# Pooled attention with a soft mixture of experts: another order for the end of the attention, and a tail in quarters of columns

## The chip, the cores and the metric

One core of a Trainium2 chip runs one program. TensorE (PE; PEld is its loading of weights) multiplies, VectorE (DVE) and ScalarE (ACT) work on its sums in PSUM and on SBUF, GpSimd (POOL) on SBUF alone, and SyncE (SP) issues the transfers. Each works through its own instructions in order; semaphores keep them in step. The metric is the device time of one execution, in microseconds (us), as the median of several.

## What is computed

The reference, cut to what matters. Eight batches of eight heads; the queries are averaged in pairs, so 576 of them meet 1152 keys. The result is a table x of 4608 rows and 512 columns, which goes through a soft mixture of 8 experts with 4 slots each.

```python
q_pool = q.reshape(B, H, S // 2, 2, D).mean(axis=3)
scores = scale * q_pool @ k.T
attn = exp(scores - scores.max(-1)); attn /= attn.sum(-1) + 1e-09
x = (attn @ v)                       # 4608 x 512
logits = x @ phi                     # 4608 x 32
d = exp(logits - logits.max(0)); d /= d.sum(0) + 1e-09
slot_input = d.T @ x                 # 32 x 512
slot_out[e] = relu(slot_input[e] @ w1[e]) @ w2[e]     # 8 experts, 4 slots each
c = exp(logits - logits.max(1)); c /= c.sum(1) + 1e-09
return c @ slot_out                  # 4608 x 512
```

All of it is in fp32.

## The kernel before

The attention runs in 96 units: 32 pairs of heads by three thirds of 192 queries. For a unit, PE makes the scores of nine blocks of 128 keys (`S`), ACT copies them, DVE takes the maximum, PE turns it (`mt`, `mb`), DVE and POOL subtract it, ACT takes exponentials, and PE multiplies with v (`av`). Three units' results of four pairs make a batch of x, `xn`.

Each of the eight batches then goes through its part of the mixture (class `Moe`): `xa` and `xb` turn `xn`, `lg` makes the logits in four groups of 32 rows, one for each pair of heads, `to` adds the groups with the matrix `SI4f` (one half holds two of the three thirds, the other the third one, so there are two `lg` and two `to`), `rm` and `nm` take the running maximum over all rows, `ex` the exponentials. `we` (method `weights`, line 803) turns these exponentials, so that they can be the stationary side of the gather: for each of the three thirds a block of 128 rows, which goes to `eA`, and a rest of 64, which is written twice, to the upper and the lower 64 partitions, and goes to the two halves of `eB`. `ga` (method `gather`, line 829) multiplies them with x, with three groups of 32 columns of the array at work at once, and adds the sum to `slot`, rescaled by `corr`. `cb`, `ce`, `cy`, `cz`, `cr` and `cm` make the combine weights `cN`.

What sets the order: every engine's instructions stand as they are issued (class `InOrder`, line 380). Up to the last `av` a planner (`graph`, `plan`) sets the order from a table of costs and due times; what is left then, the end of batch 6 (b) and all of batch 7 (a), is ordered by hand in `end` (line 353): a list of steps, each with the PSUM bank that it uses. A step with a phase 0 is PE's part, one with a phase 1 or more the copy or sum that takes it out of PSUM. Bank numbers 0 to 7 lie in four tiles of two banks; waits are kept by tile.

Behind the attention lies the tail. `pT` turns `slot` and divides it by the sums (`SIz`), DVE copies it to `sT`, and the experts run: `up` (first weights, 512 columns), `relu`, `turn_h`, `down` (second weights; four experts at once in four groups of 32 columns, twice). `down` goes by halves h of the 512 output columns. `spread` copies a half's sum and spreads it over the partitions; `give` multiplies it with the turned combine weights `cT` (made by `turn_c` in three blocks of 16) and writes pieces of 384 kB. Each `give` makes two writes. The expert weights are 64 tiles of 512 kB; NW = 28 of them have buffers of their own and are loaded during the attention, NW2 = 20 take over the attention's memory, and the last 16 take the first 16's buffers.

Of the kernel before, what the change touches and what calls it, by code (L numbers as in the profile page):

```python
# [352 lines left out]
def end(B, u):  # L353
# [10 lines left out]
        (("lg", a, 1, 0), 2), (("lg", a, 1, 1), 2),  # L364
        (("to", a, 0, 0), 0), (("rm", a, 0), None),
        (("to", a, 1, 0), 6), (("rm", a, 1), None),
        (("we", b, 0), 4), (("nm", a), None), (("we", b, 3), 4), (("ex", a), None), (("we", b, 2), 4),
        (("we", a, 0), 2), (("we", a, 2), 2), (("we", a, 3), 2),
        (("ns", a), None), (("zs",), None), (("to", a, 0, 1), 0), (("to", a, 1, 1), 6),
        (("ga", b, 0), 4), (("ga", b, 1), 4), (("ga", b, 2), 4),  # L370
        (("ga", a, 0), 2), (("ga", a, 1), 2), (("ga", a, 2), 2),
        (("cb", a, 0), 6), (("cb", a, 1), 6), (("ce", a), None), (("cy", a), None), (("cz", a), None), (("cr", a), None), (("cm", a), None),
# [3 lines left out]
NW2 = 20  # L376
NW = 28
# [18 lines left out]
def pooled_attention_soft_moe(ctx: ExitStack, tc: tile.TileContext, q, k, v, phi, w1, w2, out):  # L396
# [44 lines left out]
    cN = keep.tile([NQ, NT, NS], F32, name="cN")  # L441
    slot = keep.tile([P, DM], F32, name="slot")
# [217 lines left out]
    class Moe:  # L660
# [195 lines left out]

    pairs = [Pair(n) for n in range(B * HP)]
# [3 lines left out]
    def load_first(i):  # L861
# [19 lines left out]
        ga=lambda i, *a: M_(i).gather(*a), zs=lambda _: total_sum(), w=lambda i, _: load_first(i),  # L881
# [21 lines left out]
    cT = tl.tile([P, NT // 4, NQ], F32, name="cT")  # L903

    def turn_c(k, bank):

        for i in range(4):
            t = 16 * k + 4 * i
            pe.transpose(bank[:, i * NQ:(i + 1) * NQ], cN[:, t:t + 4, :].rearrange("p t s -> p (t s)"), ident[:NQ, :NQ])
        act.copy(cT[:, 4 * k:4 * k + 4, :], bank[:, :4 * NQ].rearrange("p (t n) -> p t n", t=4))  # L910

    pT = banks[4]
    for c in range(KC1):
        pe.matmul(pT[:, c * NS:(c + 1) * NS], slot[:, c * P:(c + 1) * P], SIz, start=True, stop=True)
    sT = tl.tile([P, KC1, NS], F32, name="sT")
    dve.tensor_copy(sT, pT[:, :KC1 * NS].rearrange("p (c s) -> p c s", c=KC1))

# [29 lines left out]
    DH = DM // 2  # L947

    def down(h, r, i, cs=range(4)):

        for c in cs:
# [5 lines left out]
    so = [tl.tile([P, DH], F32, name=f"so{h}") for h in range(2)]  # L957

    def spread(h, phase):

        if phase == 0:
            last[h] = tl.tile([P, DH], F32, name=f"last{h}")
            act.copy(last[h], banks[h][:, :DH])
        else:
            pe.matmul(banks[2 + h][:, :DH], SI4f, last[h], start=True, stop=True)
            dve.tensor_copy(so[h], banks[2 + h][:, :DH])

    last = {}

    def give(h, k, fc):  # L970

# [4 lines left out]
        for x in range(2):  # L976
            ob = ring([P, 2, 4 * NQ], F32, f"ob{h}_{k}_{fc}_{x}")
            for t in range(2):
                (act.copy if t else dve.tensor_copy)(ob[:, t], pts[2 * x + t])
# [71 lines left out]
```

## Time and profile before

| | us |
|---|---|
| median of 3 timed runs | 885.15 |
| lowest and highest | 882.51, 886.06 |
| profiled execution, own time | 887.7 |
| its span, first to last instruction | 885.9 |
| mean granted TensorE clock in the span | 0.989 |

A profile is one execution, recorded by the hardware. Busy time of an engine is the time in which one of its instructions runs; matmuls overlap, so a group's busy time ends with its last one's end. In a row of the timeline stand the start, the busy time, the engine, the operation, the tile written and those read, and how many instructions were merged; in brackets, for how long the engine had idled and what ended that. `f32` products take two passes each and count twice; turns take one. All instructions of the kernel carry line 390, that of the helper which records them, so they are told apart by tiles: `d` and `b` are PSUM, in the attention and in the tail.

### The profile page before, as it was taken

What the parts mean: (1) busy time and instruction counts of PE and PEld (TensorE: products, weight loads), DVE (VectorE), ACT (ScalarE), POOL (GpSimd) and SP (SyncE); (2) the same over time, 40 slices, a digit from 0 to 9 for tenths busy, and PEclk for the clock granted to TensorE, in tenths of its full rate; (3) what the DMA queues carried; (4) which work ended last, traced back from release to release, by engine and by line L of the source; (5) the groups of instructions that cost most, each with busy time, mean ns of one, the idle gap of its engine ahead of it and who ended that gap; (6) DMA issues with size and microseconds to landing.
All of it is one profiled execution on the core that took longest, in us unless ns stands there. A gap on an engine that the chain in (4) does not pass through costs nothing.

```text
span 885.9 us, 36358 instructions
## 1 busy us (share of the span) xinstructions
PE 844.9 (95%) x16240; PEld 705.1 (80%) x16240; DVE 745.4 (84%) x1090; ACT 754.7 (85%) x1142; POOL 351.3 (40%) x244
## 2 busy tenths in 40 slices
PE   5999999999999999999999999999999999998995
PEld 4888888887888878887888878887888878887342
DVE  5899999997999979998899979998899979995223
ACT  5899899998899989998899989998899989997123
POOL 1444444442444434443444434444344423441100
PEclk9999999999999999999999999999999999999898
DMA  6143434341333334341243332221132222217688
GB/s 166 56 130 106 130 107 130 106 131 29 117 120 104 108 104 131 107 130 29 84 126 106 107 82 82 83 82 30 56 84 82 83 63 74 72 69 277 267 330 329
DMA packets 102428, 102.08 MB, mean 115 GB/s; under 512 B 78336, under 2 KB 78848, under 8 KB 102272
## 3 DMA queue, kind: packets, MB, share of 16 engines
q1 hardware_dynamic: 102272, 99.76, 36.4%
q8 instruction: 127, 2.08, 1.0%
q14 instruction: 29, 0.24, 0.1%
HBM read 90.31 MB, written 9.44 MB: 113 GB/s over the span
## 4 chain that ended last, share of the span: by engine, by line
PE 63%; ACT 25%; issue 7%; DVE 4%; DMA 0%; SPq 0%; DVEq 0%; ACTq 0%
PE d L390 57%; ACT s L390 20%; PE b L390 5%; DVE M L390 2%; ACT mS L390 1%; ACT Us L390 1%; ACT lT L390 1%; ACT xT L390 1%; DVE s L390 1%; DMA k<-in_k_dram 0%; DVE rc L390 0%; DVE d L390 0%; DVE mc L390 0%; ACT eB L390 0%; ACT eA L390 0%
## 5 line engine op out<-in xcount | busy, mean ns | idle before, releaser
L390 PE MATMUL d<-qs,k 64*128 64x192 f32 x3456 | 367.9, 342 | 14.1 <-DMA k<-in_k_dram 5.0
L390 ACT COPY s<-d 128x768 f32<-128x768 f32 (+1 forms) x480 | 334.5, 737 | 45.5 <-PE d L390 38.8
L390 PEld LDWEIGHTS d<-v,s 128*64 128x64 f32 x10368 | 319.0, 138 | 51.3 <-issue 28.1
L390 PE MATMUL d<-v,s 128*64 128x65 f32 x10368 | 346.9, 224 | 8.5 <-ACT lT L390 5.4
L390 ACT ACTIVATE s<-s 128x1152 f32<-128x1152 f32 x288 | 328.6, 1169 | 7.1 <-DVE s L390 6.1
L390 POOL TENSOR_TENSOR s<-s,mS 128x1152 f32<-128x1152 f32 x95 | 251.8, 2651 | 196.7 <-issue 109.3
L390 PEld LDWEIGHTS d<-qs,k 64*128 64x128 f32 x3456 | 275.1, 188 | 47.7 <-ACT s L390 18.3
L390 DVE TENSOR_TENSOR s<-s,d 128x1152 f32<-128x1152 f32 x193 | 259.5, 1346 | 7.5 <-PE d L390 4.4
L390 DVE TENSOR_TENSOR M<-d,M 128x768 f32<-128x768 f32 (+1 forms) x288 | 237.1, 823 | 25.6 <-ACT s L390 11.2
L390 POOL TENSOR_TENSOR xn<-Us,rc 128x192 f32<-128x192 f32 x95 | 48.3, 508 | 171.3 <-DVE rc L390 113.2
L390 DVE TENSOR_TENSOR M<-d,s 128x768 f32<-128x768 f32 x96 | 91.0, 948 | 15.5 <-ACT s L390 14.9
L390 DVE TENSOR_TENSOR d<-d,M 128x384 f32<-128x384 f32 x96 | 54.4, 567 | 21.5 <-ACT s L390 12.3
L390 POOL TENSOR_TENSOR qs<-qs,q 128x576 f32<-128x576 f32 x31 | 44.1, 1422 | 38.4 <-DMA q<-in_q_dram 32.0
L390 DVE TENSOR_REDUCE mc<-d 128x3 f32<-128x384 f32 x96 | 52.8, 550 | 0.3 <-ACT s L390 0.3
L390 ACT COPY mS<-d 128x384 f32<-128x384 f32 x95 | 46.8, 492 | 1.2 <-DVE s L390 1.2
L390 ACT COPY Us<-d 128x195 f32<-128x195 f32 x95 | 30.9, 325 | 7.7 <-PE d L390 6.7
L390 PE MATMUL d<-ident,mc 64*128 64x64 f32 x576 | 36.9, 234 | 0.0
L390 PEld LDWEIGHTS d<-ident,M 64*128 64x128 f32 x576 | 32.8, 138 | 4.4 <-DVE M L390 1.5
L390 PE MATMUL d<-ident,M 64*128 64x64 f32 x576 | 33.9, 222 | 1.2 <-DVE M L390 1.2
L390 POOL TENSOR_TENSOR cN<-cN,cz 96x192 f32<-96x192 f32 x8 | 4.1, 507 | 72.5 <-DVE cz L390 72.5
L390 DVE TENSOR_SCALAR rc<-Us 128x3 f32<-128x3 f32 x95 | 30.6, 322 | 0.0
L390 PEld LDWEIGHTS d<-ident,mc 64*128 64x128 f32 x576 | 24.9, 133 | 7.0 <-DVE M L390 1.0
(84 smaller groups left out, 337.7 us busy)
## 6 DMA issues: line engine op xcount, KB each, us to landing
w<-in_moe_w_dram SPq DMA_DIRECT2D x64, 512.0 KB, 6.3
v<-in_v_dram SPq DMA_DIRECT2D x32, 576.0 KB, 4.8
k<-in_k_dram SPq DMA_DIRECT2D x31, 576.0 KB, 3.9
out_dram<-ob SPq DMA_DIRECT2D x24, 384.0 KB, 3.6
qs<-in_q_dram SPq DMA_DIRECT2D x31, 288.0 KB, 4.4
q<-in_q_dram SPq DMA_DIRECT2D x31, 288.0 KB, 5.1
k<-in_k_dram SPq DMA_DIRECT2D x1, 320.0 KB, 3.6
k<-in_k_dram SPq DMA_DIRECT2D x1, 256.0 KB, 3.2
```

What stands on the lines that cost most here:

```text
L390: return self.tc.keep_in_program_order(op(*args, **kwargs))
```

## The change

Three things are changed.

The 64-wide rests of `we` are no longer written by two products with the identity. One turn of 128 columns puts the rest in the upper 64 partitions (and 64 other columns in the lower), and one turn of 64 columns then writes the lower.

The list in `end` has another order and other banks. The turns of batch 6 stand between the two `lg`, with their copies on ACT; the gather of batch 6 stands between the maximum and the exponentials; the turns of batch 7 follow, then one product of the identity with itself, whose result nobody reads (`id`), and the gather of batch 7. `pT` and two blocks of `turn_c` are steps of this list now; one block stands ahead of `pT`, the combine turns `cb` and the other block behind it. `cT` and `sT` live in memory that is kept from the start, so NW is 26 and NW2 is 22.

The second half of the output columns is taken in two quarters: three sums (`PARTS`: two column blocks, one, one), each spread and given as soon as it stands.

```diff
@@ end
-        (("lg", a, 1, 0), 2), (("lg", a, 1, 1), 2),
-        (("to", a, 0, 0), 0), (("rm", a, 0), None),
...
+        (("we", b, 0), 0),
+        (("lg", a, 1, 0), 2), (("lg", a, 1, 1), 2), (("we", b, 1), 0),
...
-NW2 = 20
-NW = 28
+NW2 = 22
+NW = 26
@@ weights
                     pe.transpose(pt[:, k, :], lT[:NS, a:a + P], ident[:NS, :NS])
-                    for h in range(2):
-                        pe.matmul(pt[H * h:H * h + H, n + k, :], lT[:NS, b:b + H], ident[:NS, :NS], start=True, stop=True,
-                                  skip_group_check=True)
+                    pe.transpose(pt[:, n + k, :], lT[:NS, b - H:b + H], ident[:NS, :NS])
+                    pe.transpose(pt[:H, n + k, :], lT[:NS, b:b + H], ident[:NS, :NS])
@@ new steps of the list
+    def turn_c(k, phase, bank):
+
+        if phase == 0:
+            for i in range(4):
+                t = 16 * k + 4 * i
+                pe.transpose(bank[:, i * NQ:(i + 1) * NQ], cN[:, t:t + 4, :].rearrange("p t s -> p (t s)"), ident[:NQ, :NQ])
+        else:
+            act.copy(cT[:, 4 * k:4 * k + 4, :], bank[:, :4 * NQ].rearrange("p (t n) -> p t n", t=4))
+
+    def slots(phase, bank):
+
+        if phase == 0:
+            for c in range(KC1):
+                pe.matmul(bank[:, c * NS:(c + 1) * NS], slot[:, c * P:(c + 1) * P], SIz, start=True, stop=True)
+        else:
+            dve.tensor_copy(sT, bank[:, :KC1 * NS].rearrange("p (c s) -> p c s", c=KC1))
+
+    def turn_over(n, bank):
+
+        for i in range(n):
+            pe.matmul(bank[:, :P], ident, ident, start=True, stop=True)
@@ tail
+    PARTS = [(0, 1), (2,), (3,)]
+    acc = [banks[i] for i in (0, 1, 3)]
+    spr = [banks[2], banks[1][:, DH:], banks[3][:, DH:]]
...
+    def down(a, r, i):
+
+        n, h, f0 = len(PARTS[a]) * P, PARTS[a][0] // 2, PARTS[a][0] % 2 * P
+        for c in range(4):
             for g in range(4):
-                pe.matmul(banks[h][NS * g:NS * g + NS, :DH], hT[r][:, 4 * i + c, NS * g:NS * g + NS],
-                          wt[(4 * r + g, 1, h, i)][:, c, :], start=(r == 0 and i == 0 and c == 0),
+                pe.matmul(acc[a][NS * g:NS * g + NS, :n], hT[r][:, 4 * i + c, NS * g:NS * g + NS],
+                          wt[(4 * r + g, 1, h, i)][:, c, f0:f0 + n], start=(r == 0 and i == 0 and c == 0),
...
-    half = iter([(1, r, i, cs) for r in range(2) for i in range(2) for cs in ((0, 1), (2, 3))])
     spread(0, 0)
-    turn_c(0, banks[5])
+    turn_c(2, 0, banks[5])
+    turn_c(2, 1, banks[5])
+    down(1, 0, 0)
     spread(0, 1)
-    down(*next(half))
+    down(1, 0, 1)
     bank = Ring(banks[4:] + [banks[0], banks[2]])
-    pieces = [(k, fc) for k in range(3) for fc in range(2)]
-    for i, (k, fc) in enumerate(pieces):
-        give(0, k, fc)
-        if i in (0, 2):
-            turn_c(k + 1, bank())
-        down(*next(half))
-    down(*next(half))
+    give(0, 0, 0)
+    down(1, 1, 0)
+    give(0, 0, 1)
+    down(1, 1, 1)
+    give(0, 1, 0)
     spread(1, 0)
+    give(0, 1, 1)
     spread(1, 1)
-    for k, fc in pieces:
-        give(1, k, fc)
+    down(2, 0, 0)
+    give(0, 2, 0)
+    down(2, 0, 1)
+    give(0, 2, 1)
+    down(2, 1, 0)
+    give(1, 0, 0)
+    down(2, 1, 1)
+    spread(2, 0)
+    give(1, 1, 0)
+    spread(2, 1)
+    give(1, 2, 0)
+    for k in range(3):
+        give(2, k, 0)
```

PE before, from the second part of the first `lg` on (the four PSUM tiles of the attention are `d_126` to `d_129` before and `d_128` to `d_131` after). `xT` is x turned, `phis` and `phisB` the two layouts of phi, `lT` the logits or exponentials by slot (one for batch 6, two for batch 7), `SI` the summing matrix; `ident,lT` are turns.

```order
L390 MATMUL d_128<-xT_0_11671,phisB 32x128 x4
L390 MATMUL d_127<-xT_1_11816,phis 32x128 x4
L390 MATMUL d_127<-xT_1_11816,phisB 32x64 x4
L390 MATMUL d_126<-lT_0_11821,SI_73 128x384
L390 MATMUL d_129<-lT_1_11831,SI_73 128x192
L390 MATMUL d_128<-ident,lT_11586 128x32
L390 MATMUL d_128<-ident,lT_11586 64x32 x2
L390 MATMUL d_128<-ident,lT_11586 128x32
```

The turns of batch 6 begin behind both totals here. PE after, from the same instruction on.

```order
L392 MATMUL d_130<-xT_0_11669,phisB 32x128 x4
L392 MATMUL d_128<-ident,lT_11584 128x32 x2
L392 MATMUL d_128<-ident,lT_11584 64x32
L392 MATMUL d_128<-ident,lT_11584 128x32 x2
L392 MATMUL d_128<-ident,lT_11584 64x32
L392 MATMUL d_128<-ident,lT_11584 128x32 x2
L392 MATMUL d_128<-ident,lT_11584 64x32
L392 MATMUL d_129<-xT_1_11814,phis 32x128 x4
L392 MATMUL d_129<-xT_1_11814,phisB 32x64 x4
L392 MATMUL d_130<-lT_0_11819,SI_73 128x384
L392 MATMUL d_129<-lT_1_11838,SI_73 128x192
L392 MATMUL d_131<-xn_0_9137,eA_136 32x512
```

The turns of batch 6, with one instruction less in each third, moved from behind the two totals to between the two pairs of `lg` rows; behind the totals now stands the first product of a gather.

PE before, from the last gather's last products to the experts' first (`SIz,slot` is `pT`, `w,sT` the experts).

```order
L390 MATMUL d_127<-xn_2_10894,eB_137 32x4x64
L390 MATMUL d_129<-ident,lT_11884 96x32 x6
L390 MATMUL b_12023<-SIz,slot 128x32 x4
L390 MATMUL b_12019<-w_0_0_605,sT 32x512
L390 MATMUL b_12019<-w_0_0_837,sT 32x512
```

`pT` is the last thing ahead of the experts here, the turns of the combine logits (`ident,lT`) stand ahead of it. PE after, in the same place.

```order
L392 MATMUL d_128<-xn_2_10892,eB_139 32x4x64
L392 MATMUL d_131<-ident,cN 128x96 x4
L392 MATMUL d_131<-SIz,slot 128x32 x4
L392 MATMUL d_130<-ident,lT_11893 96x32 x6
L392 MATMUL d_129<-ident,cN 128x96 x4
L392 MATMUL b_12037<-w_0_0_607,sT 32x512
```

The six turns of the combine logits moved from ahead of `pT` to behind it, and two blocks of turns of `cN` came from the tail.

DVE before, from batch 6's `eB` copies to the `sT` copy.

```order
L390 COPY eB_136<-d_128 64x96 x2
L390 COPY eB_137<-d_127 64x96 x2
L390 TENSOR_TENSOR zs<-rsum,eps 128x1
L390 RECIPROCAL zs<-zs 128x1
L390 TENSOR_TENSOR SIz<-SI_73,zs 128x32
L390 SCALAR_TENSOR_TENSOR slot<-slot,corr_11766,d_128 96x512
L390 SCALAR_TENSOR_TENSOR slot<-slot,corr_11860,d_127 96x512
L390 TENSOR_REDUCE cm_11913<-d_129 96x6
L390 TENSOR_TENSOR cN<-d_129,cm_11913 96x192
L390 TENSOR_REDUCE cz_11917<-cN 96x6
L390 RECIPROCAL cz_11917<-cz_11917 96x6
L390 COPY sT<-b_12023 128x128
```

Both adds into `slot` and the whole combine chain (`cm` to `cz`) stand ahead of the `sT` copy here. DVE after, from the first add into `slot` on.

```order
L392 SCALAR_TENSOR_TENSOR slot<-slot,corr_11764,d_131 96x512
L392 COPY eB_139<-d_128 64x96 x2
L392 TENSOR_TENSOR zs<-rsum,eps 128x1
L392 RECIPROCAL zs<-zs 128x1
L392 TENSOR_TENSOR SIz<-SI_73,zs 128x32
L392 SCALAR_TENSOR_TENSOR slot<-slot,corr_11862,d_128 96x512
L392 COPY sT<-d_131 128x128
L392 TENSOR_REDUCE cm_11927<-d_130 96x6
L392 TENSOR_TENSOR cN<-d_130,cm_11927 96x192
L392 TENSOR_REDUCE cz_11931<-cN 96x6
```

The first add into `slot` stands ahead of batch 7's `eB` copies now, batch 6's are gone from DVE, and the `sT` copy stands directly behind the second add instead of behind the combine chain.

ACT before, from the first spread's copy on (`ob` are output pieces).

```order
L390 COPY last_12206<-b_12019 128x256
L390 COPY cT<-b_12024 128x384
L390 COPY ob_0_0_0_12227<-b_12024 128x384
L390 COPY ob_0_0_1_12231<-b_12026 128x384
L390 COPY cT<-b_12019 128x384
L390 COPY ob_0_1_0_12252<-b_12023 128x384
L390 COPY ob_0_1_1_12256<-b_12025 128x384
L390 COPY ob_1_0_0_12272<-b_12019 128x384
L390 COPY ob_1_0_1_12276<-b_12023 128x384
L390 COPY cT<-b_12024 128x384
L390 COPY ob_1_1_0_12297<-b_12026 128x384
```

Three `cT` copies stand between the output copies here, and the next `last` copy comes six rows further on. ACT after, from the same copy on.

```order
L392 COPY last_12052<-b_12037 128x256
L392 COPY cT<-b_12042 128x384
L392 COPY ob_0_0_12265<-b_12042 128x384
L392 COPY ob_0_1_12269<-b_12044 128x384
L392 COPY ob_0_0_12293<-b_12039 128x384
L392 COPY ob_0_1_12297<-b_12042 128x384
L392 COPY ob_1_0_12321<-b_12044 128x384
L392 COPY ob_1_1_12325<-b_12039 128x384
L392 COPY last_12053<-b_12038 128x128
L392 COPY ob_1_0_12334<-b_12042 128x384
L392 COPY ob_1_1_12338<-b_12044 128x384
```

Two of the three `cT` copies are gone from between the output copies, and a `last` copy of a quarter stands after the sixth `ob` copy.

## Rows read from the trace of the kernel before

**Rows 1.** Windows: busy time (instructions) of each engine, PEclk, DMA share, GB/s.

```profile
814.20:817.80 3.60, 2.65 (x23) 1.79 (x20) 1.71 (x6) 1.51 (x7) 0.00 (x0) 1.00 0.97 356
817.80:824.60 6.80, 6.80 (x42) 2.88 (x44) 1.77 (x6) 1.71 (x8) 0.00 (x0) 0.50 0.92 352
824.60:828.00 3.40, 2.45 (x29) 1.61 (x23) 1.71 (x4) 0.51 (x2) 0.00 (x0) 1.00 0.69 269
828.00:831.40 3.40, 2.81 (x16) 0.79 (x20) 0.35 (x2) 0.15 (x1) 2.29 (x3) 0.51 0.00 0
```

**Rows 2.** Timeline from 813 to 826: the last logits to the slots.

```profile
813.69 0.40 PE L390 MATMUL d<-xT,phis 128*32 128x128 f32 x8
813.90 0.32 PE L390 MATMUL d<-xT,phisB 128*32 128x64 f32 x8
...
814.47 1.24 PE L390 MATMUL d<-lT,SI 128*128 128x384 f32 x4 [0.25 <-ACT lT L390]
...
815.64 1.29 PE L390 MATMUL d<-ident,lT 32*128 32x32 f32 x15
...
817.63 1.78 PE L390 MATMUL d<-ident,lT 32*128 32x32 f32 x15 [0.70 <-ACT lT L390]
...
819.46 0.24 ACT L390 COPY eA<-d 128x96 f32<-128x96 f32 x1 [1.35 <-PE d L390]
...
819.73 0.53 DVE L390 COPY eB<-d 64x96 f32<-64x96 f32 x2 [2.16 <-ACT eA L390]
...
825.64 0.74 DVE L390 SCALAR_TENSOR_TENSOR slot<-slot,corr,d 96x512 f32<-96x512 f32 x1 [1.84 <-PE d L390]
```

**Rows 3.** Timeline from 826 on: slots, experts, first output.

```profile
826.44 1.08 PE L390 MATMUL b<-SIz,slot 128*128 128x32 f32 x8 [0.47 <-DVE slot L390]
...
828.29 0.25 DVE L390 COPY sT<-b 128x128 f32<-128x128 f32 x1
...
828.59 10.18 PE L390 MATMUL b<-w,sT 128*32 128x512 f32 x80 [1.07 <-DVE sT L390]
...
853.36 0.55 PE L390 MATMUL b<-ident,cN 96*128 96x96 f32 x4
...
854.55 0.59 PEld L390 LDWEIGHTS b<-w,hT 128*32 128x32 f32 x16 [0.33 <-issue]
854.55 1.07 PE L390 MATMUL b<-w,hT 128*32 128x256 f32 x16
...
855.55 0.93 PE L390 MATMUL b<-cT,so 32*128 32x384 f32 x8
...
857.12 24.97 SPq L390 DMA_DIRECT2D out_dram<-ob  x24
```

**Rows 4.** DMA engines from 850 to 886: 40 slices' busy tenths, GB/s.

```profile
DMA  9999410019969998999999700799999999999940
GB/s 396 432 382 391 178 55 0 18 68 386 399 246 399 393 396 335 362 393 399 386 380 395 283 38 14 307 393 406 396 396 389 403 403 389 406 396 396 393 171 0
```

**Rows 5.** Timeline of PE in batch 0: six equal turns, then the turns of `we`.

```profile
214.90 0.46 PE L390 MATMUL d<-ident,lT 32*96 32x32 f32 x6
...
215.30 0.92 PE L390 MATMUL d<-qs,k 64*128 64x192 f32 x8
...
217.03 0.24 PE L390 MATMUL d<-ident,lT 32*128 32x32 f32 x1
...
217.20 0.48 PE L390 MATMUL d<-ident,lT 32*64 32x32 f32 x5
...
217.43 0.42 PE L390 MATMUL d<-ident,lT 32*128 32x32 f32 x3
...
218.25 2.32 PE L390 MATMUL d<-v,s 128*64 128x65 f32 x72
```

**Rows 6.** Timeline of PE in batch 0: the gather at full clock.

```profile
222.00 1.06 PE L390 MATMUL d<-xn,eA 128*32 128x512 f32 x6 [0.26 <-ACT Us L390]
...
223.86 0.43 PE L390 MATMUL d<-qs,k 64*128 64x192 f32 x2
```

More of the change, by code (lines that the diff above doesn't have):

```diff
@@ L441, in pooled_attention_soft_moe @@
     cN = keep.tile([NQ, NT, NS], F32, name="cN")
+    cT = keep.tile([P, NT // 4, NQ], F32, name="cT")
+    sT = keep.tile([P, KC1, NS], F32, name="sT")
     slot = keep.tile([P, DM], F32, name="slot")
@@ L880, in pooled_attention_soft_moe @@
         cr=lambda i, _: M_(i).crec(), cm=lambda i, _: M_(i).cmul(), we=lambda i, *a: M_(i).weights(*a),
-        ga=lambda i, *a: M_(i).gather(*a), zs=lambda _: total_sum(), w=lambda i, _: load_first(i),
+        ga=lambda i, *a: M_(i).gather(*a), zs=lambda _: total_sum(),
+        ct=lambda k, ph, b: turn_c(k, ph, single[b]), pT=lambda ph, b: slots(ph, single[b]), id=lambda n, b: turn_over(n, single[b]), w=lambda i, _: load_first(i),
     )
@@ L902, in pooled_attention_soft_moe @@
     banks = [ps.tile([P, 512], F32, name=f"b{i}", tag=f"b{i}") for i in range(8)]
[L903 to L916, printed above, removed]
     hT = [tl.tile([P, KC2, P], F32, name=f"hT{r}") for r in range(2)]
@@ L947, in pooled_attention_soft_moe @@
     DH = DM // 2
-    def down(h, r, i, cs=range(4)):
-        for c in cs:
+    PARTS = [(0, 1), (2,), (3,)]
+    acc = [banks[i] for i in (0, 1, 3)]
+    spr = [banks[2], banks[1][:, DH:], banks[3][:, DH:]]
+    so = [tl.tile([P, len(p) * P], F32, name=f"so{i}") for i, p in enumerate(PARTS)]
+    last = [tl.tile([P, len(p) * P], F32, name=f"last{i}") for i, p in enumerate(PARTS)]
+    def down(a, r, i):
+        n, h, f0 = len(PARTS[a]) * P, PARTS[a][0] // 2, PARTS[a][0] % 2 * P
+        for c in range(4):
@@ L959, in spread @@
-    def spread(h, phase):
+    def spread(a, phase):
+        n = len(PARTS[a]) * P
         if phase == 0:
-            last[h] = tl.tile([P, DH], F32, name=f"last{h}")
-            act.copy(last[h], banks[h][:, :DH])
-        else:
[L965 to L970, printed above, removed]
+            act.copy(last[a], acc[a][:, :n])
+        else:
+            pe.matmul(spr[a][:, :n], SI4f, last[a], start=True, stop=True)
+            dve.tensor_copy(so[a], spr[a][:, :n])
@@ L972, in give @@
+    def give(a, k, x):
+        fc = PARTS[a][x]
         pts = [bank()[:, :4 * NQ] for _ in range(4)]
         for t in range(4):
-            pe.matmul(pts[t], so[h][NS * t:NS * t + NS, fc * P:fc * P + P], cT[NS * t:NS * t + NS, 4 * k:4 * k + 4, :],
+            pe.matmul(pts[t], so[a][NS * t:NS * t + NS, x * P:x * P + P], cT[NS * t:NS * t + NS, 4 * k:4 * k + 4, :],
                       start=True, stop=True, tile_position=(NS * t, 0))
-        for x in range(2):
-            ob = ring([P, 2, 4 * NQ], F32, f"ob{h}_{k}_{fc}_{x}")
+        for y in range(2):
+            ob = ring([P, 2, 4 * NQ], F32, f"ob{fc}_{k}_{y}")
@@ L978, in give @@
             for t in range(2):
-                (act.copy if t else dve.tensor_copy)(ob[:, t], pts[2 * x + t])
-            sp_q.dma_start(out[h, fc, k, x].rearrange("p (t n) -> p t n", t=2), ob)
+                (act.copy if t else dve.tensor_copy)(ob[:, t], pts[2 * y + t])
+            sp_q.dma_start(out[fc // 2, fc % 2, k, y].rearrange("p (t n) -> p t n", t=2), ob)
     for c in range(KC1):
```

17 lines of the change are left out of this document (9 added, 8 removed).

## The prediction

> **What bounds the kernel now.** I read the page's slices first: PE, DVE and ACT are busy nearly throughout until the last few, so the change can only pay in the end and in the step that every batch repeats. Then the windows over the end, for the granted clock; the timeline of the end, for who waits for whom; the strip of the DMA engines under the output; and last single instructions in a batch in the middle.
>
> The windows [rows 1] are to be read by their PEclk column. From 814.2 to 817.8 PE is busy for 2.65 us of 3.60, in 23 short instructions, and after that the clock is at 0.50, the lower of its two levels (1.2 instead of 2.4 GHz), until 824.6. There it has been busy without a gap, and it is at 1.00 again. From 824.6 to 828.0 PE is busy for 2.45 of 3.40, and the next window is at 0.51.
>
> The timeline [rows 2] says what those stretches are. After the last logits (`lg`, at 813.69) come their totals (`to`, 814.47), then on DVE and ACT the maximum and the exponentials, while PE has only the turns of batch 6 (`we b`, 815.64, x15) to do; the turns of batch 7 (`we a`) begin when the exponentials end, at 817.63. Both gathers follow, all at the half clock, and the second add into `slot` starts at 825.64. The rest [rows 3]: `slot` is turned at 826.44 (`pT`), copied at 828.29 (`sT`), and the expert stage starts at 828.59 (call it U). The `sT` copy is not late because of PE, which has finished at 827.52; on DVE it stands in order behind the reciprocal of the last combine weights.
>
> In the tail the writes bound. The strip [rows 4] has slices of 0.9 us. The first write is issued at 857.12; from the slice at 858.1 on the DMA engines are full, except for 0.4 of a slice at 859.9, 0.3 at 869.8, two whole slices to 872.5 and 0.3 of the next: 2.7 us in all. At 396 GB/s a write of 393 kB takes 0.99 us, 24 take 23.8. The hole at 870 is where the first half's pieces have run out and the second half's sums are only being spread.
>
> **64-wide turns.** `we` loses two-pass products: 15 passes become 9, in eight batches, six of them (0 to 5) inside the stretch where PE has no slack. By count, 6 of 15 passes of 1.22 us (217.03 to 218.25) [rows 5] would be 0.49 us a batch, 2.9 in six. Single rows say otherwise. The 128-wide pass at 217.03 is followed by a 64-wide one at 217.20, 0.17 later; four 64-wide passes and the way back to the next 128-wide one, at 217.43, take 0.23. Six passes of one shape take 0.065 each (214.90 to 215.30). So the price is in going from one tile shape to another and back, three times, and the new order (128, 128, 64) still does so: 0.065 + 0.17 + 0.15 = 0.39 for each third, where it was 0.41. I take 0.06 a batch, **0.4 us** in six, since it is built from the row of this very step. The bounds: 2.9 gained by count; lost, a further switch of 0.17 in each of 18 thirds, 3.1. The Trainium skill (TensorEngine Tiling (Array Packing), Tiling Modes, Restrictions) says that column tiling switches off transpose mode for fp32 input, and these 64-wide turns are just that; by it they would run as two-pass products, nothing would be won here, and the sum below would be 0.4 us worse; no run of this trace has such an instruction.
>
> **Between the logits' stages.** `we b` now stands between the two `lg`. PE is free for it at 813.69, with 0.1 for the switch; at 1.2 us it puts the second `lg` at 814.97, and `lg` itself (0.21 and 0.15 for its two parts, 0.1 to switch) puts `to` at 815.42, 0.95 us later than now. From `to` to `we a` the chain keeps its 3.16 us (814.47 to 817.63) [rows 2]: `we a` at 818.58. The gather of batch 6 moves into this shadow. It starts when `to` lets go of PE (1.17 us after its start, 816.6), and at full clock it takes 1.75 us (222.00 to 223.86, less the switch) [rows 6], done at 818.35: all hidden, with 0.2 us to spare. Its `eA` and `eB` copies are ACT's now, between the `lT` copy and the exponentials, where ACT waits for DVE; they are done by 816.4. At the half clock the gather would end at 820.1, and 1.5 us of it would show.
>
> `we a`, 1.2 us, ends at 819.75. Now comes a wait that was not there: nothing is left to cover the copies of batch 7's weights (`eA` on ACT, then two `eB` on DVE; 819.46 to 820.26, 0.8 us), and the new gather uses the bank that they read. It starts at 820.7; PE has one dummy product of two passes in that gap, for which I count nothing. The gather takes 1.75, the add into `slot` starts at 822.55. Behind the waiting PE stands only the turn of the first combine weights, and on SP the last two weight loads that need the attention's memory, which waited for the other gather so far.
>
> What would the old order give at full clock? 817.63 + 1.2 + 2 x 1.75 + 0.1 = 822.45. **So at one clock the new order wins nothing here.** What it wins is that PE has products to run where it now idles, and the 3.2 us to 825.64 are lost to the clock alone.
>
> **From slot to the experts.** `pT` 0.80 after the add starts (825.64 to 826.44): 823.35; it takes 1.08, and `sT`, ahead of the combine chain on DVE now, starts at 824.45 instead of waiting 0.77 us. PE, though, gets 6 turns of the combine weights (0.39 + 0.1) and 4 of the first `cT` block (0.41 + 0.1; 0.55 with its drain at 853.36) after `pT`, so the experts start at 825.3 rather than at 824.8. Gain at U: **3.3 us**. If the clock is up there too, the 2.8 us of half clock at the start of the experts (828.59 to 831.4) cost nothing: **1.4 us** more. From U to the end of the first half's sums the work is as before (24.77 us, so 23.35 at full clock): X, now 853.36, becomes 848.65. Two more weight tiles are loaded after the attention instead of during it, some 1.3 us each (524 kB at 400 GB/s); the DMA engines are empty from 828.0 to 831.4 (share 0.00) [rows 1], where these fit. The sixteen loads that wait for the experts to free their slots begin near 828 then and take 21 us, until 849, some 3 us before the last is used. I count nothing; without that cover it would be 2.6 us.
>
> **The tail in quarters.** From X to the first output piece PE now does a turn, one half piece and the sum's spread: 2.19 us (853.36 to 855.55). It will do the turn, a quarter, the spread and a second quarter. A quarter is 4 x 8 passes of 128 columns. The row of that shape is `lg`: 8 passes in 0.21 (813.69 to 813.90), so 0.87 a quarter and 0.13 to switch: the first write comes 1.0 later after X. In return two turns leave the tail, and the second and third sums are ready while the writes run: 2.5 of the 2.7 idle us go. Is the supply fast enough? A piece (0.93, at 855.55) and a quarter (1.0) take 1.93 us and give two writes, 1.98 us. Just. Net **1.6 us**; other bound below.
>
> Sum: 0.4 + 3.3 + 1.4 + 1.6 = 6.7 us, against the profiled execution's own time 887.7 (span 885.9 and 1.8 around): 881.0. The median of the timed runs is 2.55 under that time. Part of this will be clock that they did not lose and cannot win back, so I carry over only 1.5: **879.5 us**.
>
> **The rivals.** *The clock falls all the same.* For: PE still idles from 819.8 to 820.7 but for the dummy, and from 822.5 to 825.3 it has only short turns and `pT`, much like the two stretches after which it fell. Against: the long idle stretch of `to` to `we a` is now filled with a gather. One fall costs about 1.6 us (881.1 timed); falls in both places give the old clock, the gather of batch 7 at 3.4 us, `we a` 0.5 longer and the slow start of the experts, 3.6 to 3.9 in all: 883.3. I take 882.
>
> *The tail becomes PE's: the slower side.* A quarter has as many passes as a whole piece had, with half the columns. If the weights of a pass of four groups (0.59 us for four such, so 0.15 (PEld at 854.55) [rows 3]) do not lie under the pass before (0.107), a quarter takes 8 x 0.257 = 2.05 us. Two quarters stand ahead of the first write, six more between writes; with about 1.1 us of slack that is 8 x 1.18 - 1.1 = 8.3 us lost against my sum: 889.3, or 887.8 timed, slower than before. It is slower than now from 1.7 us a quarter on. Against it speaks `lg`, with the same weights, columns and four groups. The Trainium skill (TensorEngine Tiling (Array Packing), Instruction Overhead) puts about 60 cycles on every matmul, whatever its columns; estimated from that, 16 added passes a quarter at 25 ns would cost 0.4 us each, 2.1 in all, and the sum would come to 881.6 timed.
>
> *The turns pay by count*: 2.5 us beyond my 0.4, 877.0. *The turns do not do what they say*: two passes, or one switch more; 880 to 883.
>
> **How the numbers follow.** Forecast 879.5 with 0.47; the clock falls 0.30; by count 0.12; PE's tail 0.06; slower turns 0.05. Half a per cent of 885.15 is 4.4 us, about what a measurement of this kernel can tell from no change: under 880.7 is faster, over 889.6 slower. Faster: most of the forecast (0.40), all of the count, a quarter of the falls, a little more: 0.61. Slower: PE's tail with a fall on top, 0.04. Same: 0.35. The range reaches from the count's case to past both falls, 876.5 to 884.0.
>
> **What would show it.** PEclk at 1.00 from 817.8 on, and the gather of batch 6 ending before `we a` starts; a `we` in the middle of 1.15 us or so and not 0.75; `sT` directly behind `pT`; U near 825; a quarter under 1.1 us; no empty slice between the first write and the last. Wrong if the clock falls before the experts, if `we` has moved by half a microsecond, or if the first write comes later than 5 us after X.

## The result, and the profile after

The changed kernel takes 877.54 us (median of five, 875.55 to 878.65) against 885.15; the ratio is 0.9915 with an interval of 0.9891 to 0.9939. That is 7.6 us less; the forecast was 879.5, the range 876.5 to 884.0. The profiled execution took 877.61 us, its span is 875.8, and its mean granted clock 0.994.

By stretches of the two profiled executions (U is the experts' start, X the first turn of `cN` behind the first half's sums, as in the prediction):

| stretch, us | before | predicted | after |
|---|---|---|---|
| start to the last `av` | 811.4 | 811.0 | 806.9 |
| first `lg` of the end to U | 15.58 | 12.3 | 11.52 |
| U to X | 24.77 | 23.35 | 23.37 |
| X to the first write | 3.76 | 4.76 | 4.70 |
| first write to the end | 28.8 | 26.2 | 27.7 |
| span | 885.9 | 879.2 | 875.8 |

Two rows are wrong by much, and in opposite directions: the first, where the six `we` stand, and the fifth, the writes.

The windows over the end of the changed kernel (columns as in [rows 1]):

```profile
808.48:811.50 3.02, 3.02 (x48) 2.02 (x47) 0.23 (x1) 2.13 (x8) 0.14 (x1) 1.00 0.90 324
811.50:816.20 4.70, 3.97 (x37) 1.87 (x38) 2.75 (x10) 2.77 (x10) 0.00 (x0) 1.00 0.99 377
816.20:820.00 3.80, 3.43 (x38) 2.51 (x32) 1.34 (x3) 0.45 (x1) 0.00 (x0) 1.00 1.03 414
820.00:823.40 3.40, 3.40 (x33) 1.06 (x36) 0.94 (x4) 1.07 (x4) 1.54 (x3) 1.00 1.01 405
```

PEclk stays at 1.00 from the logits into the experts; in [rows 1] it was 0.50 in two of four. The timeline of the same stretch, which answers to [rows 2] and the head of [rows 3]:

```profile
808.48 0.64 PE L392 MATMUL d<-xT,phis 128*32 128x256 f32 x8
...
809.27 0.65 PE L392 MATMUL d<-ident,lT 32*128 32x32 f32 x9
...
810.32 1.24 PE L392 MATMUL d<-lT,SI 128*128 128x384 f32 x4
...
811.49 1.06 PE L392 MATMUL d<-xn,eA 128*32 128x512 f32 x6
...
813.54 0.74 DVE L392 SCALAR_TENSOR_TENSOR slot<-slot,corr,d 96x512 f32<-96x512 f32 x1 [0.99 <-PE d L392]
...
813.62 0.74 PE L392 MATMUL d<-ident,lT 32*128 32x32 f32 x9 [0.21 <-ACT lT L392]
814.34 0.49 PE L392 MATMUL d<-ident 128*128 128x128 f32 x2
...
815.34 1.06 PE L392 MATMUL d<-xn,eA 128*32 128x512 f32 x6 [0.52 <-ACT rsum L392]
...
817.31 0.74 DVE L392 SCALAR_TENSOR_TENSOR slot<-slot,corr,d 96x512 f32<-96x512 f32 x1 [1.44 <-PE d L392]
818.11 1.08 PE L392 MATMUL d<-SIz,slot 128*128 128x32 f32 x8 [0.37 <-DVE slot L392]
...
819.23 0.29 DVE L392 COPY sT<-d 128x128 f32<-128x128 f32 x1 [1.17 <-PE d L392]
...
820.00 1.50 PE L392 MATMUL b<-w,sT 128*32 128x512 f32 x12
```

The gather of batch 6 (811.49) lies between the totals and `we a`, which waits only 0.21 us for the exponentials. The gather of batch 7 waits 1.0 us behind `we a` (the new wait, of which the dummy product fills half; the profile puts its end down to ACT's `rsum`, done 0.06 us after the `eB` copies), and `sT` stands directly behind `pT`. But `we` takes 0.58 us (809.27 to 809.85) and not 1.2. So it does in a middle batch, which answers to [rows 5]:

```profile
217.14 0.65 PE L392 MATMUL d<-ident,lT 32*128 32x32 f32 x9
217.72 0.69 PE L392 MATMUL d<-v,s 128*64 128x65 f32 x16
```

0.58 to the next work instead of 1.22: 0.64 us saved in each batch. The shift of the last products with v against before grows in steps of 0.64 at each of the six `we`, 3.8 us; the remaining 0.7 of the 4.5 us are single steps elsewhere. The largest, 0.6 between 459 and 462, the two kernels of forms below gain on the kernel before as well, with other `we`: it is a delay in the one profiled execution of before, no gain of the change.

The tail, with the first row of [rows 3]'s end again and the quarter's length:

```profile
843.37 0.55 PE L392 MATMUL b<-ident,cN 96*128 96x96 f32 x4
...
843.85 0.81 PEld L392 LDWEIGHTS b<-w,hT 128*32 128x32 f32 x32
843.85 1.08 PE L392 MATMUL b<-w,hT 128*32 128x128 f32 x32
...
844.86 0.70 PE L392 MATMUL b<-last,SI 128*128 128x256 f32 x2
...
846.50 0.93 PE L392 MATMUL b<-cT,so 32*128 32x384 f32 x8
...
848.07 22.64 SPq L392 DMA_DIRECT2D out_dram<-ob  x24
```

A quarter piece takes 1.01 us (843.85 to 844.86), as predicted; its weight loads (0.81) lie under it. The DMA engines from 840 to 876, in slices of 0.9 us (as [rows 4]):

```profile
DMA  9999941000999999999889999999999999998100
GB/s 414 401 414 410 350 178 50 18 0 38 393 403 393 396 396 399 389 382 397 314 314 391 403 396 393 389 407 369 399 410 396 396 403 406 393 399 314 44 10 0
```

No empty slice between the first write and the last. Yet 1.3 us of what that should bring are missing at the end. The last 6 us before, from 880 on, in slices of 0.15 us:

```profile
DMA  9999999999999899999999999999995000000000
```

And the last 6 us after, from 870 on:

```profile
DMA  9999899999999989998952111100100000000000
```

Before, all 16 engines stop together at 884.7. After, most stop at 873.1, three go on, and one until 874.6: by the landings of the last write, its slowest engine is 1.44 us behind the middle one, where before it was 0.10.

### The profile page after: what moved, and what is told of

Its sections match the earlier page's. It is cut to its first block, busy times and chain, and to the rows that moved or that the text cites. A ratio compares the mean times of both kernels' runs of the same rounds, so it can differ in the third digit from the quotient of the medians.

```text
span 875.8 us, 36527 instructions
## 1 busy us (share of the span) xinstructions
PE 836.6 (96%) x16324; PEld 704.6 (80%) x16324; DVE 744.9 (85%) x1089; ACT 755.2 (86%) x1145; POOL 350.8 (40%) x244
## 4 chain that ended last, share of the span: by engine, by line
PE 61%; ACT 28%; issue 7%; DVE 3%; DMA 0%; SPq 0%; DVEq 0%; ACTq 0%
PE d L392 55%; ACT s L392 22%; PE b L392 5%; ACT mS L392 2%; ACT Us L392 1%; DVE M L392 1%; ACT lT L392 1%; ACT xT L392 1%; DVE s L392 0%; DMA k<-in_k_dram 0%; ACT eB L392 0%; DVE d L392 0%; DVE mc L392 0%; ACT eA L392 0%; DVE rc L392 0%
## 5 line engine op out<-in xcount | busy, mean ns | idle before, releaser
L392 DVE TENSOR_TENSOR M<-d,M 128x768 f32<-128x768 f32 (+1 forms) x288 | 237.1, 823 | 25.7 <-ACT s L392 11.9
L392 DVE TENSOR_TENSOR d<-d,M 128x384 f32<-128x384 f32 x96 | 54.4, 567 | 17.6 <-ACT s L392 8.4
L392 PE MATMUL d<-ident,M 64*128 64x64 f32 x576 | 33.9, 222 | 1.2 <-DVE M L392 1.2
```

The lines of the kernel that those rows point to most:

```text
L392: return self.tc.keep_in_program_order(op(*args, **kwargs))
```

## Experiments

### The new turns alone, the tail in halves, and the changed kernel again

First the kernel before with only the new turns.

```diff
-                    for h in range(2):
-                        pe.matmul(pt[H * h:H * h + H, n + k, :], lT[:NS, b:b + H], ident[:NS, :NS], ...)
+                    pe.transpose(pt[:, n + k, :], lT[:NS, b - H:b + H], ident[:NS, :NS])
+                    pe.transpose(pt[:H, n + k, :], lT[:NS, b:b + H], ident[:NS, :NS])
```

> The kernel before with the new turns of the 64-wide rests alone. Theory 1 (what costs in `we` is the way from a turn to a product and back; turns among themselves cost nothing extra, whatever their width): `we` in a middle batch takes 0.58 us instead of 1.22, the first `lg` of the end comes 6 x 0.64 = 3.9 us earlier (near 809.1 instead of 813.01), the two `we` of the end save another 1.2; median near 880.2, ratio 0.994. Theory 2 (the price is in going from one tile shape to another, as the prediction had it): `we` 1.15 us, the first `lg` near 812.6, median near 884.5, ratio 0.999. By both the clock falls in the end as before, and from the first `lg` to the experts it takes 14.3 us or more (15.58 before, 11.52 after).

881.37 us, ratio 0.9965 (0.995 to 0.9979). The first `lg` comes at 808.25, 4.8 us earlier, and `we` takes 0.58: far from the prediction's 1.15. From `lg` to U it is 13.50 us, less than expected, since the clock falls once instead of twice (windows):

```profile
808.20:813.20 5.00, 3.41 (x53) 2.32 (x51) 1.63 (x6) 2.83 (x11) 0.19 (x1) 1.00 0.94 327
813.20:816.60 3.40, 3.40 (x22) 1.36 (x23) 1.02 (x5) 1.55 (x7) 0.00 (x0) 0.50 1.01 410
816.60:821.70 5.10, 3.61 (x38) 2.02 (x32) 2.81 (x7) 0.66 (x2) 0.09 (x1) 1.00 0.96 359
```

By its median it is 1.2 us slower than expected, and its profile shows 1.3 us more in the tail: X to the end takes 33.86 us with the very code that took 32.56 before. The slowest engine ends 1.41 us behind here too, so quarters are not its cause.

Next the changed kernel with the old tail in halves (two blocks of turns still out of it).

```diff
-    PARTS = [(0, 1), (2,), (3,)]
+    DH = DM // 2   # down, spread, give by halves, as before
-    down(1, 0, 0)
     spread(0, 1)
-    down(1, 0, 1)
+    down(*next(half))
```

> The changed kernel with the tail in halves again (two of the three blocks of turns stay in the attention's end). By the prediction's sum the quarters win: X to the end of the span is 32.54 less 1.0 us for the two blocks of turns, 31.5 us here, against 30.9 with quarters. By the theory that a write which a late DMA engine finishes ends the program, the quarters lose: they close the hole in which a DMA engine that was set back by an instruction fetch catches up. Then it is 31.5 us here against the 32.43 us measured with quarters, the first write comes 3.8 us after X instead of 4.7, there is a hole of about 1.5 us between the halves, and the 16 DMA engines finish the last write within 0.2 us of each other instead of 1.45. Time: 876.6 by this theory, 878.1 by the first (877.54 for the changed kernel).

878.5 us, 0.9932 (0.9914 to 0.995). X to the end is 33.03 us, the hole between the halves 1.55, and the slowest engine 1.52 behind: the second theory falls. The hole did bring the engines together, from 1.0 us to 0.11, but the next fetch came behind it. With nearly the same lateness at the end in both, quarters are 0.65 us better than halves by the profiles, the 0.6 that the prediction's sum gave; the medians of this comparison, 878.5 and 878.31 for the changed kernel, do not tell them apart.

> The changed kernel once more, for the scatter. If the late DMA engines at the end come from instruction fetches at set places of the program, the fetches come again some 13, 20 and 29 us before the end, X to the end is 32.4 us within 0.3, and the last write's slowest engine is again 1.3 to 1.6 us behind the others. If they were chance, it differs by 0.5 us or more. From the first `lg` to the experts 11.5 us, PEclk 1.00 throughout. Median 877.5 within 1.

878.31 us, 0.9928 (0.9909 to 0.9948). X to the end 32.31, the last engine 1.35 behind. The fetches of TensorE's instructions came 28.4, 19.5 and 11.9 us before the end, in the first profile 28.7, 19.6 and 11.9: set places, no chance. It was run once more with the last experiment below (878.47, 32.32 us, 1.40 behind).

### What a `we` is made of

Two kernels, each with six forms of `we`, one in each of the batches 0 to 5; the lines show one of the forms, and `prod` is a product with the identity. Four forms of the second kernel leave out one of the two copies of the 64-wide rest.

```diff
+                if self.b == 1:      # grouped: turns of all thirds, then products
+                    for o, x in A: pe.transpose(o, x, I)
+                    for _, lo, hi, _, x in R: prod(lo, x); prod(hi, x)
```

> The kernel before, with another form of `we` in each of the batches 0 to 5; what is read is how long `we` takes in each, from its first instruction to the next one on PE that is not part of it. Theory 1 (what costs is the way from a turn to a product, 0.17, and back, 0.15; instructions of one kind follow each other at 0.03 to 0.08 whatever their width). Theory 2 (time goes by the number of passes, 1.22 us for 15). Theory 3 (the price is in the change between 128 and 64 columns, as the prediction had it). Batch 0, as before, 15 passes: 1.22 by all. Batch 1, the three 128-wide turns first, then all products, 15 passes: 0.85 by theories 1 and 3, 1.22 by 2. Batch 2, products alone, 18 passes: 0.9 by theory 1, 1.46 by 2, 1.4 by 3. Batch 3, the new form, 9 passes: 0.58 by 1, 0.73 by 2, 1.15 by 3. Batch 4, the new form with the three 64-wide turns last: 0.58 by 1, 0.73 by 2, 0.7 by 3. Batch 5, per third a 128-wide turn, a 64-wide turn and a 64-wide product, 12 passes: 1.15 by theories 1 and 3, 0.98 by 2.

> The kernel before with six further forms of `we` in the batches 0 to 5, read like the first six. In batches 0, 1, 3 and 5 one copy of the 64-wide rest is left out. The two theories left after the first six: A, a product into 64 columns costs about 0.11 on the way in and 0.09 on the way out beyond the pass itself, wherever it writes and whatever stands ahead; B, the price belongs to the two products that run side by side in two column positions. Batch 0, per third a 128-wide turn and one 64-wide product into the lower partitions (9 passes): 0.97 us by A, 0.5 by B. Batch 1, the same into the upper partitions: 0.97 by A, 0.5 by B (if only the upper position costs, 0.97 here and 0.5 in batch 0). Batch 2, the three 128-wide products first, then the six 64-wide ones (18 passes): 1.3 by A, since there is one way in and one out, against 1.70 when they alternated; by B 1.5 or more. Batch 3, three 128-wide turns, then three 64-wide turns (6 passes): 0.4 by both. Batch 4, two 128-wide turns and a 64-wide product into the lower partitions (12 passes): 1.15 by A, 0.65 by B. Batch 5, a 128-wide turn and a 128-wide product (9 passes): 1.0 by both; 1.3 or more if the way between turn and product has a price of its own.

| per third (T turn, P product) | passes in a `we` | us |
|---|---|---|
| T128, P64 low, P64 high (before) | 15 | 1.22 |
| all T128 first, then all P64 | 15 | 0.77 |
| P128, P64 low, P64 high | 18 | 1.70 |
| all P128 first, then all P64 | 18 | 1.25 |
| T128, T64, P64 high | 12 | 1.30 |
| T128, T128, P64 low | 12 | 1.39 |
| T128, P64 low | 9 | 1.20 |
| T128, P64 high | 9 | 1.20 |
| T128, P128 | 9 | 0.97 |
| T128, T128, T64 (after) | 9 | 0.58 |
| all T128 first, T64 last | 9 | 0.58 |
| all T128 first, one T64 each | 6 | 0.40 |

`low` and `high` are the lower and the upper 64 partitions. Two rows of PE's timeline each, the `we` and what follows it (their difference can be off by 0.01 by rounding). Products alone, 18 passes, in the first kernel:

```profile
417.58 1.77 PE L390 MATMUL d<-ident,lT 32*128 32x32 f32 x18
419.28 0.51 PE L390 MATMUL d<-v,s 128*64 128x65 f32 x10
```

T128 with one P64, 9 passes, in the second kernel:

```profile
215.65 1.27 PE L390 MATMUL d<-ident,lT 32*128 32x32 f32 x9
216.86 0.45 PE L390 MATMUL d<-v,s 128*64 128x65 f32 x8
```

The new form, 9 passes, in the first kernel:

```profile
519.06 0.65 PE L390 MATMUL d<-ident,lT 32*128 32x32 f32 x9
519.65 0.45 PE L390 MATMUL d<-v,s 128*64 128x65 f32 x8
```

The count of passes says nothing: nine take 1.20 or 0.58. The way between turn and product is not it either: products alone are dearest, and T128 with P128 alternates three times at the pace of its passes (0.06 a turn, 0.11 a product's pass). What is left is theory A. Into a 64-wide product it takes 0.17 where the next turn would come after 0.06, out of it 0.15 where the next such product would come after 0.05, wherever it writes. What stands ahead does not matter either: behind a 128-wide product it comes after 0.20 instead of 0.11, behind a 64-wide turn after 0.12 instead of 0.03, 0.09 or 0.1 more each time. (Its sum for nine passes, 0.97, had left out the 0.08 between the two passes; 0.17 + 0.08 + 0.15 is 0.40 a third, 1.20.) A 64-wide turn has no such price: 0.06 to it, 0.03 from it.

### The order of the end at one clock

The kernel before with the new turns, its old order, and products that nobody reads in two waits.

```diff
-        (("we", b, 0), 4), (("nm", a), None), ...
+        (("we", b, 0), 4), (("id", 5), 3), (("nm", a), None), ...
-        (("cb", a, 0), 6), (("cb", a, 1), 6), ...
+        (("cb", a, 0), 6), (("id", 2), 1), (("cb", a, 1), 6), ...
```

> The kernel before with the new turns (as e1_turns) and its old order at the end, but with five products of the identity behind the turns of batch 6, where PE idles until the exponentials end, and two ahead of pT; nobody reads them. Theory 1 (the order itself wins nothing, all of it was the clock): PEclk stays at 1.00, both gathers take 3.6 us together instead of 6.9, and from the first `lg` to the experts it takes 11.8 us, against 11.5 in the changed kernel; with 1.4 us less at the start of the experts the time is 4.0 us under that of e1_turns. Theory 2 (the new order hides a gather that the old one shows, whatever the clock): with PEclk at 1.00 it still takes 13.3 us or more. If the clock falls in spite of the products, it is 14.3 us and the run says nothing on the two.

879.52 us, 0.9947 (0.9929 to 0.9966). The clock holds, by the windows from the first `lg` to U:

```profile
808.00:812.00 4.00, 3.75 (x53) 2.77 (x53) 1.50 (x6) 1.83 (x7) 0.16 (x1) 1.00 0.89 310
812.00:816.00 4.00, 3.97 (x42) 2.13 (x43) 1.85 (x7) 2.51 (x11) 0.00 (x0) 1.00 1.01 401
816.00:819.90 3.90, 2.88 (x33) 2.12 (x27) 2.12 (x7) 0.66 (x2) 0.09 (x1) 1.00 1.03 412
```

From `lg` (808.01) to U (819.95) it is 11.94 us with the old order, 11.52 with the new. In these profiles, seven useless products in the old order are worth 1.56 of the 1.98 us that the new one saves against the new turns alone (13.50). The rest, 0.4 us, is the order's own. The median is 1.9 us under that of the new turns alone, and not 4.0 as expected: from U to X both profiles take 23.37 us or 0.01 more, so there was no fall to win back, and the tail is late again (34.02 us from X, see below).

Over all profiles the fall in the gathers goes with the old order: the four without such products (the kernel before, the new turns alone, the two kernels of forms) have it, the eight with the new order have none and take 11.5 us from `lg` to U. How much falls varies. The two kernels of forms have the old order and the old `we` here, and take 14.14 and 14.19 us to the kernel before's 15.58, with one fall of 3.4 us in place of 6.8; and from U to X the clock holds in them. The first one's windows, the fall and then U to X:

```profile
815.90:819.30 3.40, 3.40 (x22) 1.16 (x23) 1.03 (x5) 1.40 (x5) 0.00 (x0) 0.50 1.03 416
824.26:847.63 23.37, 23.37 (x272) 10.10 (x272) 1.67 (x16) 2.39 (x4) 2.14 (x3) 1.00 0.87 341
```

Then the changed kernel without its one such product.

```diff
-        (("we", a, 3), 2), (("id", 1), 7),
+        (("we", a, 3), 2),
```

> The changed kernel without the one product of the identity between the turns of batch 7 and its gather, so that PE idles for 1.0 us there instead of 0.5. If that product keeps the clock up, PEclk falls to 0.50 behind it, the gather of batch 7 takes 3.4 instead of 1.85 us, and from the first `lg` to the experts it is 12.8 us or more. If the gather of batch 6 in the former idle stretch is enough, PEclk stays at 1.00 and it is 11.5 us as before.

879.52 us in a single run; `lg` to U takes 11.51, but the clock falls right behind U, 820.4 to 823.8, and U to X takes 25.07 instead of 23.37. That alone would look as if the product held the clock. A third profile of the changed kernel says otherwise; in its windows the clock fell there too, with the product in place:

```profile
812.00:818.90 6.90, 5.81 (x57) 3.74 (x51) 3.09 (x9) 2.73 (x10) 0.00 (x0) 1.00 1.02 413
819.40:822.80 3.40, 3.40 (x24) 0.83 (x20) 0.53 (x2) 0.66 (x3) 2.02 (x3) 0.50 0.93 372
```

U to X was 25.07 there, 23.37 in its two other profiles. So this fall, 1.7 us, comes in some executions and not in others (in three of the eight profiles with the new order), and what the product does is open.

### The engine that ends late

The changed kernel with TensorE's program 200 instructions longer from the start.

```diff
+    for i in range(50):
+        pe.matmul(single[7][:NS, :1], zz, zz[:, :1], start=True, stop=True)
```

> The changed kernel with 50 products of one column at the very start (nobody reads them), which makes TensorE's program 200 instructions longer ahead of everything else. Theory 1 (TensorE's instructions come in blocks of 256; each block's fetch takes about 1 us of one DMA engine and puts its share of the writes back by 2 us; the end waits for the slowest): the last two fetches move from 29 and 12 us before the end... that is, from 12 and 19 to about 18 and 26 us before the end, none comes later, the engine set back has a dozen more writes and the short hole near the tenth write to catch up, and the last write's slowest engine is 0.5 to 0.8 us behind the others instead of 1.35 to 1.45; X to the end 31.6 us instead of 32.35. Theory 2 (it is not the fetches): the last write's slowest engine is 1.35 us behind or more, and X to the end is 32.3 us or more. What the products cost at the start is not looked at.

877.88 us in a single run. X to the end is 31.91 us instead of 32.3 to 32.4, and the last engine about 1.2 behind: the right way, half the size. The fetches did move (30.9, 26.6, 17.6 us before the end). The DMA queues (packets, MB, share) from 859 to the end in the changed kernel; q8 carries TensorE's instructions, 128 packets for 32.6 thousand:

```profile
q1 hardware_dynamic: 2070, 5.62, 85.0%
q8 instruction: 1, 0.02, 0.3%
q14 instruction: 1, 0.01, 0.1%
```

And from 859 to the end in this one, without a fetch on q8:

```profile
q1 hardware_dynamic: 2156, 5.88, 87.1%
q14 instruction: 1, 0.01, 0.1%
```

Over all profiles the picture is one. The write that follows a fetch (one packet of 16 KB, 0.93 us) in the midst of others has one engine 1.5 to 2.15 us behind, mostly 1.9 or more, and 1.2 to 1.6 at the edge of a hole; without a gap it regains some 0.06 us a write (1.97 to 1.44 in nine writes of the changed kernel), and a long hole behind the fetch gives it all back. The old tail, the same code in five profiles with a hole of 2.3 us each, sorts by it. In the kernel before and the two kernels of forms the last fetch came 17.9, 17.2 and 14.6 us before the end, ahead of the hole or in it: 32.56, 32.59 and 32.54 us from X, and about 0.1 late at the end. With the new turns alone it came at 11.3, behind the hole, and with the filled waits at 14.5, running on into the first write behind it: 33.86 and 34.02 us, 1.41 and 1.56 late. Why 0.93 us of packet cost 2 us is open.

### A version that begins to write earlier

Before the first write the DMA engines idle for three slices even so. The first half in two quarters as well:

```diff
-    PARTS = [(0, 1), (2,), (3,)]
+    PARTS = [(0,), (1,), (2,), (3,)]
```

> The changed kernel with the first half in two quarters as well: four sums, the first output piece behind the first quarter. Theory 1 (the DMA engines are the tail's bound, and they idle for 3 us between the last weight load, near 845.3, and the first write at 848.07): the first write is issued near 845, the writes follow the loads without a hole but for one or two of 0.5 to 1 us where PE has not got the next quarter's sum ready, the last ends near 870.5, the span is 871 to 873 and the time 873 to 875. Theory 2 (PE, with 2 x 0.5 us of sums more and the quarters' 1.0 us for half the columns of a 1.86 us piece, becomes the bound of the tail): several holes of over 1 us, span 875 or more, no faster than the changed kernel.

876.72 us, 0.9902 (0.9884 to 0.9919). Its interval overlaps that of the changed kernel (0.9891 to 0.9939), so a gain over it is not shown. X stands behind the first quarter's sums here, and U to X is 21.66 us. The first write comes at 845.65, 2.4 us earlier, with a fall of the clock at U (1.7 us) in this profile; four holes, 0.35 to 1.0 us, are PE's, which runs with hardly a pause from 836 to 862. Both theories have a part: the early write is the first one's, the holes and the span, 875.6, are the second one's.

Then the last quarter's products ahead of two of the third quarter's outputs, and more products in the waits:

```diff
-        (("we", a, 3), 0), (("id", 1), 7),
+        (("we", a, 3), 0), (("id", 3), 7),
-        (("ct", 0, 0), 7), (("pT", 0), 6),
+        (("ct", 0, 0), 7), (("id", 1), 5), (("pT", 0), 6),
...
-        down(3, 1, 0); down(3, 1, 1); spread(3, 0); give(2, 2, 0); spread(3, 1)
+        down(3, 1, 0); give(2, 1, 0); down(3, 1, 1); spread(3, 0); spread(3, 1); give(2, 2, 0)
```

> Four quarters as in e8_q4, with the last quarter's pieces ahead of two of the third quarter's outputs, and three products of the identity instead of one ahead of the last gather and one more ahead of pT, in waits that are there anyway. Theory 1 (in e8_q4 the sums of the last quarter came too late by the 0.87 us that PE waited for them, and the fall of the clock at the experts' start is held off by the products): PEclk is at 1.00 from the first `lg` to the last product, from U to X it is 20.0 us instead of 21.66, the first write comes near 844.0, the last ends near 871.5, span 872.5 to 873.5, time 874.3 to 875.3, 2 to 3 us under the changed kernel in this same comparison. Theory 2 (the clock's falls there come whatever stands in those waits): U to X 21.6, span 874.5, time 876.3.

> The changed kernel beside e9_q4b on the same chip. 877.5 to 878.3 as in the two measurements so far; X to the end 32.35 us, the last write's slowest engine 1.35 to 1.45 us behind, the last fetch of TensorE's instructions 11.9 us before the end. If PEclk falls at the experts' start here too, U to X is 25.0 us instead of 23.38, and the one product does not decide it.

875.56 us (874.25 to 877.42), 0.9885 (0.986 to 0.9911), beside 878.47 (876.74 to 880.02), 0.9923 (0.9899 to 0.9947), for the changed kernel on the same chip. U to X takes 19.96 (21.66 in the version before it), at full clock; whether the added products held it, one profile cannot tell. Its span, 875.6, misses the forecast by 2 to 3 us: its attention ended 1.7 us later than in the first profile of the changed kernel, and three holes of 0.7 to 0.8 us stayed. It is 2.9 us under the changed kernel by the medians, with intervals that still overlap, so the gain is likely but not shown.

## Why the prediction was right, and where it was wrong

The time lay in the range and the side was right, but the sum reached it by errors of opposite sign, and that they cancelled was luck. Against the forecast of 879.5 us the turns gave 3.4 more, single steps elsewhere 0.7, the way to U 0.8; the tail gave 1.4 less and the carry-over 1.4 less: 877.4, where 877.5 was measured.

- **64-wide turns, 0.4 us: wrong, 3.8.** The failed step is "the price is in going from one tile shape to another and back, three times, and the new order (128, 128, 64) still does so". The first half stands: the price of the old `we` was the change into the 64-wide products and out of them, 0.40 a third with one product or two. The second half does not: a 64-wide turn changes nothing, and a third takes 0.19. One row held both differences, width and kind, and I put the price on width alone. The rival by count came out nearest in time (877.0) and has the wrong mechanism; by count it would be 0.73 a `we`, and nine passes can take 1.20. The Trainium skill's rule (TensorEngine Tiling (Array Packing), Restrictions), that column tiling switches off transpose mode for fp32 input, did not bite: the trace shows nine instructions in a `we`, one for each turn, the 64-wide one at 0.03 us.
- **First `lg` to U, 3.3 us: 4.1.** The two `we` on this path gave 1.1 more, waits of some 0.1 to 0.2 took 0.3 back. The rest held: the gather in the shadow, the new wait of 1.0 us (0.95 predicted), `sT` behind `pT`. But 1.4 us of it are the second stretch at the lower clock in the one profile of the kernel before; against the 14.14 and 14.19 us of the kernels of forms the changed kernel is 2.6 to 2.7 better.
- **"At one clock the new order wins nothing": right within 0.4 us** (11.94 against 11.52). The rival in which the clock falls all the same did not come in the gathers; behind U it came in one of three profiles of this kernel.
- **U to X, 1.4 us: right where the clock holds** (23.37 for 23.35), nothing where it falls (25.07). It is no gain of the change, though: in the four other profiles with the old order the clock held there too (23.37 or 23.38), and only the profiled execution of the kernel before fell.
- **Tail, 1.6 us: wrong, 0.2.** Its parts held: first write 4.70 us behind X (4.76), a quarter piece 1.01 (1.00), weights hidden, and 2.46 of 2.5 idle us recovered, by the write's middle engine. By the Trainium skill (TensorEngine Tiling (Array Packing), Instruction Overhead), with its 60 cycles on every matmul, a quarter would by the prediction's estimate have been 0.4 longer; the trace, with 1.01, does not bear it out here. What the sum lacked is a term: the slowest engine, 1.34 us later than before. In [rows 4] the hole hid it; I counted the hole as pure loss, and it was where a set-back engine caught up (1.77 us late ahead of it, 0.10 behind it).
- **Carry-over, 1.5 us: wrong, 0.1.** The profiled execution of before stood 2.55 us over its median. The sum took 1.5 of that off again for the timed runs of after, whose profiled execution stood only 0.07 over theirs. The reason given, clock that the timed runs did not lose, was right and counted for too little: the falls that the kernels of forms do not have are 1.4 us ahead of U and 1.4 behind it, together a little more than the 2.55. No second profile of the kernel before shows it directly. But of its 36 timed runs beside the experiments 33 had a higher mean clock than the profiled one's 0.989, and the other three took 887.7 to 888.1 us as it did.

## What to carry to other kernels

Price a change of instruction from a row in which it alone differs: here the one row mixed width and kind, and a kernel with six forms in six equal batches settled it in one run. Before an idle hole is counted as gain, ask what recovers in it. Where a gain comes with a reordering, fill the old order's waits with useless work once: it tells the order from the clock. And take more than one profile of the kernel before: here the only one had lost 2.8 us of clock that its neighbours kept, and the sum counted them as gain.

## What was not expected of the hardware

A fetch of TensorE's instructions, 16 KB and 0.93 us on one DMA engine, puts that engine's share of a stream of writes back by some 2 us, and the same tail took 32.6 or 33.9 to 34.0 us by where in the program the fetch fell. A 128-wide turn and a 64-wide product behind it take 0.40 us together, and a second such product beside the first adds nothing; 64-wide turns among 128-wide ones cost no more than their pass, 0.03 to 0.06. And the same program's clock fell at the experts' start in one profile of three.
